# A long-convolution and token-mixing kernel: an inverse transform centred in time, half sums shared by mirrored outputs, and 16-bit sine and cosine

## Chip, cores and metric

The kernel runs on one core of one Trainium2 chip. The metric is the device time of one execution in microseconds (us); shorter is better. Engines are called by the profile's names: PE (TensorE, its weight loads shown apart as PEld), DVE (VectorE), ACT (ScalarE), POOL (GpSimd) and SP (SyncE, which here only issues DMAs).

## What is computed

Two steps follow each other, for a batch of B = 8 sequences of S = 5696 tokens with D = 128 channels:

```
Xf = rfft(x, n=2*S, axis=1); Hf = rfft(h, n=2*S, axis=0)
y  = irfft(Xf * Hf[None], n=2*S, axis=1)[:, :S]         # causal convolution, each channel by itself

theta = y @ w_theta                                     # 128 x 128
zr, zi = y * cos(theta), y * sin(theta)
m = einsum('ts,bsd->btd', w_tok_r, zr) + einsum('ts,bsd->btd', w_tok_i, zi)   # two 5696 x 5696 matrices
u = y + m
out = u + relu(u @ w_ch)
```

## The kernel before

**Three parts in time.** First comes a set-up of tables and the transform of h, to about 55 us in the profile. Then the convolution is done in eight groups (two sequences times 64 channels each), to about 400 us. The last part, from about 410 us, is the mixing with the two token matrices.

**Stages of a group.** A 2S-point transform is split into factors of 89 or 90 and 64.

- Stage A: matmuls L242 (180 columns) with evictions L251 on ACT and L249 on DVE.
- Stage B: twelve chunks. `f2` (L262, L268) makes the spectrum of a chunk in PSUM; ACT casts it to the tile `xs` (L398); DVE multiplies it by the transform of h, the tile `hs`, in one product of 2048 elements, to `uv_t` (L400; the smaller last chunk in two, L405). `hs` is loaded by SP from the DRAM tensor `hf_hbm` (`load`, L391): four loads lead (`LEAD = 4`), and load c + 4 is issued after product c. `uv_t` is what stage C has as weights, in the halves `u_t` and `v_t`.
- Stage C: 16 chunks of 8. Each of the 128 results is a matmul with `u_t` as weights and the table `r_u` streaming (L421), added to one with `v_t` and `r_v` (L422), 128 columns each. A chunk of 1024 columns is evicted to the tile `g` in 16 bits, with a sign per row (`sgn`) on one part: by DVE in one multiplication (L429), or by ACT in two operations (L426, L427), which it does for four of the chunks (eight in the last group).
- Stage D: 64 outputs, two matmuls each (L444, 89 columns, weights from `g`, streaming the table `e_t`). Chunks of 10 outputs are evicted to the tile `yt` by DVE (L448, two chunks) or ACT (L450). The result is stored to `yt_hbm` (L457).

**Order.** `woven` merges lists of steps, each list spread over a share of the stage. Stage C of group g is woven with stage A of group g + 1 (over 0 to 0.7) and with the loads of x for group g + 2 on POOL's queue; stage D of group g is woven with stage B of group g + 1. So two kinds of stages alternate: "C", with A in it, and "B/D". Engines take their instructions in that order. In group 0, the set-up of the rest of the tables (`e_table`) is woven in as well.

**Phases.** `phases_b` makes theta, its sine and cosine, and the products zi and zr. There are 44 steps for rows that come straight from the transform, woven into the last group and following it (`phase_step`, with `turns`), and 46 more, later, among the mixing. In a step, ACT takes the absolute value (L539), the sine (L540) and the cosine of the absolute value (L541), and DVE multiplies (L552, L553). The steps of the transform's rows make a bf16 copy on DVE (L704), which is stored.

**Mixing.** The token matrices are loaded in pieces by POOL's queue (L630), transposed on DVE (L842), partly added (L851), and used in matmuls L1227, L1148 and L1114, with sums on DVE (L1234). Partial results go through DRAM (`cp_hbm`, stored at L977).

Of the kernel before, what the change touches and what calls it, by code (L numbers as in the profile page):

```python
# [10 lines left out]
F32 = mybir.dt.float32  # L11
BF16 = mybir.dt.bfloat16
F16 = mybir.dt.float16
# [4 lines left out]
TWO_PI = 2.0 * math.pi  # L18
# [4 lines left out]
def kernel(  # L23
# [68 lines left out]
    hf_hbm = nc.dram_tensor("hf_hbm", (NCK, 2, N2, 2, HD * CK), F16, kind="Internal").ap()  # L92
# [68 lines left out]
    for n, (col, per) in enumerate(((1, N1), (0, NF), (0, N2), (1, NF))):  # L161
        nc.vector.tensor_scalar(lane[:, n + 2:n + 3], lane[:, col:col + 1], 1.0 / per, None, op0=mult)
# [42 lines left out]
    sign = fc.tile([P, 1], F32)  # L205

# [77 lines left out]
    k_r = index([[0, 2], [1, N2]], "k_r")  # L284
    t_r = []
    for n in range(2):
        t_r.append(s1.tile([P, P], F32, tag=f"t_r{n}", name=f"t_r{n}"))
        for q0 in range(2):
            for q1 in range(2):
                rows, cols = slice(64 * q0, 64 * q0 + 64), slice(64 * q1, 64 * q1 + 64)  # L290
                nc.gpsimd.tensor_scalar(t_r[n][rows, cols], k_r[rows, cols], of_r[rows], 0.25 * (1 + n + q0 - q1),
                                        op0=mult, op1=add)
    for f in load_x(1):
        f()
    e_flat = fc.tile([P, EN * 2 * NB], F16, name="e_t")
# [4 lines left out]
    nc.gpsimd.iota(e_f[1], pattern=[[1, 11], [N2, NB]], base=0, channel_multiplier=0,  # L300
# [4 lines left out]
    signs()  # L305
    pad = v_t[:, 5 * D * CK:6 * D * CK]
# [28 lines left out]
    def h_chunk(c):  # L335
        c0, ck = CHK[c]
        ps = f2(a_h, c, 0)
        h_ = hst[c // 6][:, c % 6]
        dst = h_[:, :, :, :ck]
        if c in (0, 2, 5, 7, 10):  # L340
            nc.vector.tensor_scalar(dst, ps, 16.0 / NF, None, op0=mult)
        else:
            nc.scalar.activation(dst, ps, AF.Copy, scale=16.0 / NF)
        for cc, j in ((0, 0), (NCK - 1, CHK[-1][1] - 1)):
            if c == cc:
                nc.vector.tensor_scalar(dst[:, :, :, j], dst[:, :, :, j], 0.5, None, op0=mult)
        for ri in range(2 if c % 3 == 2 else 0):
            nc.sync.dma_start(
                hf_hbm[c - 2:c + 1, :, :, ri, :].rearrange("c h p n -> p (c h) n"),
                hst[c // 6][64 * ri:64 * ri + 64, c % 6 - 2:c % 6 + 1].rearrange("p c h d k -> p (c h) (d k)"))  # L350

    r_u = fc.tile([P, P], F16)
    r_v = fc.tile([P, P], F16)
    sgn = fc.tile([P, N2], F32)

    def r_table(n_, r_):
        k = within(t_r[n_], s1.tile([P, P], F32, tag=f"k_r{n_}", name=f"k_r{n_}"))
        sine(k, t_r[n_], 1)
        return lambda: (
            nc.vector.tensor_scalar(r_[:, :N2 + EN], k[:, :N2 + EN], 0.125, None, op0=mult),  # L360
            nc.vector.tensor_scalar(r_[:, N2 + EN:], k[:, N2 + EN:], -0.125, None, op0=mult))
# [14 lines left out]
    def s_table():  # L376
        nc.vector.memset(sgn, 1.0)
        nc.vector.tensor_scalar(sgn[:, EN:], sgn[:, EN:], sign, None, op0=mult)
# [3 lines left out]
    def stage_b(a_st, dh, warm=WARM):  # L382

        hs_of = {}

        def load(c):
            if c >= NCK:
                return
            hs = hs_of[c] = fh.tile([P, 2, HD * CK], F16, tag="hs", name="hs")
            for e in range(2):  # L390
                nc.sync.dma_start(hs[64 * e:64 * e + 64], hf_hbm[c, dh])  # L391

        def chunk(c):
            c0, ck = CHK[c]
            hv = hs_of[c].rearrange("p r (d k) -> p r d k", k=CK)
            ps = f2(a_st, c, warm)
            xs = fs.tile([P, 2, HD, CK], F16, tag="xs", name="xs")
            nc.scalar.activation(xs[:, :, :, :ck], ps, AF.Copy)  # L398
            if ck == CK:
                nc.vector.tensor_tensor(  # L400
                    uv[:, :, :, c0:c0 + ck],
                    xs.rearrange("p e d k -> p e (d k)").unsqueeze(1).to_broadcast([P, 2, 2, HD * CK]),
                    hv.rearrange("p r d k -> p r (d k)").unsqueeze(2).to_broadcast([P, 2, 2, HD * CK]), op=mult)
            for r in range(2 if ck < CK else 0):
                nc.vector.tensor_tensor(  # L405
                    uv[:, 2 * r:2 * r + 2, :, c0:c0 + ck], xs[:, :, :, :ck],
                    hv[:, r:r + 1, :, :ck].to_broadcast([P, 2, HD, ck]), op=mult)
            load(c + LEAD)
        return [lambda c=c: load(c) for c in range(LEAD)], [lambda c=c: chunk(c) for c in range(NCK)]

    def stage_c(st, last):
        sg = sgn[:K1].unsqueeze(2).unsqueeze(1).to_broadcast([K1, 2, N2, 8])

        def chunk(q):
# [3 lines left out]
            for i in range(8):  # L418
# [3 lines left out]
                nc.tensor.matmul(o, v_t[:, at:at + P], r_v, start=False, stop=True)  # L422
            g_out = st["g"][:K1, :, q:q + 8].rearrange("p (r n) q -> p r n q", r=2)
            g_in = ps[:K1].rearrange("p a (q r n) -> p r n (a q)", q=4, r=2)
            if q % 16 == 0 and (last or q >= 64):
                nc.scalar.activation(g_out[:, :, :EN], g_in[:, :, :EN], AF.Copy)  # L426
                nc.scalar.mul(g_out[:, :, EN:], g_in[:, :, EN:], sgn[:K1, EN:EN + 1])  # L427
            else:
                nc.vector.tensor_tensor(g_out, g_in, sg, op=mult)  # L429
        return [lambda q=q: chunk(q) for q in range(0, 2 * HD, 8)]  # L430

    def stage_d(st, bp, dh, then=None):
        def chunk(n0, cn):
# [5 lines left out]
            for j in range(cn):  # L439
                n = n0 + j  # L440
                o = ps[:, j // nq, (j % nq) * NB:(j % nq + 1) * NB]
                for ri in range(2):
                    e_ = e_t[:K1, n, ri, :] if n < EN else e_t[:K1, N2 - n, ri, ::-1]
                    nc.tensor.matmul(o, g_[:K1, ri * N2 + n, :], e_, start=(ri == 0), stop=(ri == 1))  # L444
# [30 lines left out]
    r_rest = [lambda: rr.extend([r_table(0, r_u), r_table(1, r_v)]), lambda: rr[0](), lambda: (rr[1](), s_table())]  # L475
# [30 lines left out]
    def phases_b(ti, y_ap, b0, nb, yT, sb, th_pool, th_tag, zi_eng, turns=None, tags=("red", "mag"), m=P,  # L506
# [5 lines left out]
        red = sb.tile([P, n], F32, tag=(tags or ("red", "mag"))[0], name="red")[:m]  # L512
        mag = sb.tile([P, n], F32, tag=(tags or ("red", "mag"))[1], name="mag")[:m]
        y_ap = y_ap[:m]
        if turns is None:
# [8 lines left out]
        else:  # L524
            ones, plus, minus, w_neg = turns
# [13 lines left out]
        nc.scalar.activation(mag, r, AF.Abs)  # L539
        nc.scalar.activation(red, r, AF.Sin, bias=zero_b[:m], scale=-TWO_PI)  # L540
        nc.scalar.activation(mag, mag, AF.Sin, bias=half_pi[:m], scale=-TWO_PI)  # L541
# [7 lines left out]
        else:  # L549
            zi = red.bitcast(BF16)[:, :n]  # L550
            zr = mag.bitcast(BF16)[:, :n]
        zi_eng.tensor_mul(zi, red, yflat)  # L552
        nc.vector.tensor_mul(zr, mag, yflat)  # L553
# [172 lines left out]
    for g, (bp, dh) in enumerate(groups):  # L726
# [12 lines left out]
        woven((c_, 0.06 if a_ else 0.0, 1.0), (a_, 0.0, 0.7), now, load_, (load_x(g + 2, st), 0.1, 1.02))  # L739
# [550 lines left out]
```

## Time and profile before

| | |
|---|---|
| median of 3 runs | 2061.07 us (2054.74 to 2062.02) |
| profiled execution: span | 2056.1 us (no whole time is given beside it) |
| PE, DVE, ACT, POOL busy | 95%, 77%, 31%, 47% |
| mean granted TensorE clock | 0.99 |
| stage C of the groups 1 to 4, first L421 to last L422 | 19.1, 19.1, 19.1, 20.1 us |
| stage B/D between them | about 19 us |

Times are those of one execution from the start of its span. A line as "L400 DVE" is line 400 of the kernel. A matmul's duration includes its way through the array, so the pace of a stream of matmuls is read from the starts.

### The profile page before, as it was taken

To read this page: it belongs to the slowest core of one execution; us is meant where nothing else is said; L and a number is where in the kernel's file an instruction comes from. 1 tells how busy PE (TensorE), PEld (TensorE's weight loads), DVE (VectorE), ACT (ScalarE), POOL (GpSimd) and SP (SyncE) were. 2 spreads that over 40 slices of the span, in tenths; PEclk is the share of its full clock that TensorE was granted. 3 is DMA by queue.
4 is the path that set the end of the run, shared out by engine and by line. 5 is a ranking of instruction groups with operands and counts; after the bars stand their busy time and mean duration, and the time that the engine had idled before them with its cause. 6 is when DMAs were issued, how large, how long until landed. Compare 5 with 4: busy or idle time off the path is not lost.

```text
span 2056.1 us, 41703 instructions
## 1 busy us (share of the span) xinstructions
PE 1951.6 (95%) x15757; PEld 1077.6 (52%) x15933; DVE 1579.0 (77%) x2802; ACT 640.1 (31%) x972; POOL 969.0 (47%) x1766
## 2 busy tenths in 40 slices
PE   7789889789999999999999998999999999999998
PEld 5688878654444444444444443444444444444444
DVE  7777778777788888888867667867777686777767
ACT  6778777862332333333300000011111111111111
POOL 8323412385354545445476454454544535354450
PEclk9899999999999999999999999999999999999999
DMA  9899987999899998989899799687887969788783
GB/s 156 125 158 168 148 161 215 235 271 199 164 171 183 166 180 157 178 167 184 163 174 163 118 246 222 104 153 132 148 147 128 155 127 153 131 150 146 133 153 86
DMA packets 504250, 335.02 MB, mean 163 GB/s; under 512 B 184759, under 2 KB 457271, under 8 KB 503063
## 3 DMA queue, kind: packets, MB, share of 16 engines
q0 software_dynamic: 322368, 157.47, 59.9%
q1 hardware_dynamic: 175696, 163.33, 27.5%
q10 hardware_dynamic: 5984, 11.54, 1.6%
q8 instruction: 125, 2.05, 0.4%
q14 instruction: 77, 0.63, 0.1%
HBM read 376.39 MB, written 92.49 MB: 228 GB/s over the span
## 4 chain that ended last, share of the span: by engine, by line
PE 60%; DVE 5%; DMA 4%; POOL 2%; issue 2%; ACT 0%; DVEq 0%; ACTq 0%; POOLq 0%; SPq 0%
PE m L1227 56%; POOL ring L630 2%; DVE c L1234 2%; DMA ring<-in_moe_w_tok_i_dram 2%; DVE b L783 1%; PE v L929 1%; PE utp L922 1%; DMA b<-z_hbm 1%; PE m L1231 1%; DVE wt L842 1%; DMA ring<-in_moe_w_tok_r_dram 1%; PE theta_ps L517 0%; PE tpz L870 0%; DMA yT<-yt_hbm 0%; PE m L1114 0%
## 5 line engine op out<-in xcount | busy, mean ns | idle before, releaser
L630 POOL DMA_DIRECT2D ring<-in_moe_w_tok_i_dram x720 | 387.9, 546 | 662.4 <-DVE wt L842 567.0
L630 POOL DMA_DIRECT2D ring<-in_moe_w_tok_r_dram x720 | 386.5, 548 | 149.8 <-DVE wt L842 84.7
L842 DVE STREAM_TRANSPOSE wt<-ring 128x384 f32<-128x384 f32 (+2 forms) x720 | 358.7, 522 | 116.4 <-PE m L1227 69.5
L1227 PE MATMUL m<-b,wt 128*128 128x512 bf16 x1605 | 386.6, 380 | 3.8 <-DVE wt L842 1.7
L1227 PEld LDWEIGHTS <-wt 128*128 128x128 bf16 x1804 | 176.4, 98 | 219.8 <-DVE wt L842 7.5
L1234 DVE TENSOR_TENSOR c<-c,m 128x512 f32<-128x512 f32 x412 | 264.9, 668 | 0.4 <-PE m L1227 0.4
L924 ACT ACTIVATE ring<-utp 128x512 bf16<-128x512 bf16 x85 | 50.8, 597 | 582.2 <-PE utp L922 582.2
L421 PE MATMUL ps<-r_u,uv_t 128*128 128x128 f16 x1024 | 125.6, 219 | 9.1 <-DVE uv_t L405 3.0
L422 PE MATMUL ps<-r_v,uv_t 128*128 128x128 f16 x1024 | 124.6, 219 | 1.3 <-issue 0.9
L400 DVE TENSOR_TENSOR uv_t<-xs,hs 128x2048 f16<-128x2048 f16 x88 | 105.7, 1224 | 23.4 <-ACT xs L398 12.5
L1148 PE MATMUL m<-b,wt 128*128 128x512 bf16 x471 | 111.6, 383 | 10.1 <-DVE wt L842 4.9
L919 ACT ACTIVATE ub<-c 128x512 bf16<-128x512 f32 x88 | 55.1, 628 | 193.0 <-DMA ring<-in_moe_w_tok_r_dram 114.6
L146 POOL DMA_DIRECT2D x<-in_x_dram x128 | 99.6, 786 | 22.6 <-POOL x L144 13.3
L422 PEld LDWEIGHTS <-uv_t 128*128 128x128 f16 x1024 | 100.0, 98 | 9.3 <-issue 7.7
L398 ACT ACTIVATE xs<-ps 128x1024 f16<-128x1024 f32 x96 | 91.7, 977 | 37.8 <-DVE uv_t L400 23.0
L421 PEld LDWEIGHTS <-uv_t 128*128 128x128 f16 x1024 | 100.1, 98 | 4.5 <-DVE uv_t L405 4.3
L1148 PEld LDWEIGHTS <-wt 128*128 128x128 bf16 x528 | 50.5, 98 | 67.5 <-DVE wt L842 7.3
L519 ACT ACTIVATE red<-theta_ps,magic 128x512 f32<-128x512 f32 (+1 forms) x46 | 31.6, 687 | 135.7 <-PE theta_ps L517 106.6
L262 PEld LDWEIGHTS <-w_t 64*128 64x128 f16 x3240 | 58.1, 99 | 29.2 <-issue 21.7
L872 ACT ACTIVATE ring<-tpz 128x512 bf16<-128x512 bf16 (+1 forms) x46 | 27.5, 597 | 130.4 <-PE tpz L870 114.9
L541 ACT ACTIVATE mag<-mag,half_pi 128x512 f32<-128x512 f32 (+1 forms) x90 | 65.1, 723 | 0.0
L242 PE MATMUL ps<-f_t,x 89*128 89x180 f16 x512 | 60.3, 252 | 2.3 <-DVE a L249 1.2
(2929 smaller groups left out, 3758.7 us busy)
## 6 DMA issues: line engine op xcount, KB each, us to landing
ring<-in_moe_w_tok_r_dram POOLq DMA_DIRECT2D x352, 96.0 KB, 4.3
ring<-in_moe_w_tok_i_dram POOLq DMA_DIRECT2D x352, 96.0 KB, 4.8
ring<-in_moe_w_tok_r_dram POOLq DMA_DIRECT2D x352, 80.0 KB, 4.4
ring<-in_moe_w_tok_i_dram POOLq DMA_DIRECT2D x352, 80.0 KB, 3.8
hs<-hf_hbm SPq DMA_DIRECT2D x192, 128.0 KB, 3.4
cp_hbm<-c SPq DMA_DIRECT2D x88, 256.0 KB, 2.3
c<-cp_hbm SPq DMA_DIRECT2D x88, 256.0 KB, 4.2
out_dram<-c SPq DMA_DIRECT2D x88, 256.0 KB, 4.2
```

What stands on the lines that cost most here:

```text
L146: nc.gpsimd.dma_start(x16[p0:p1, e, n0:n0 + 16, :HD], bass.AP(tensor=src.tensor, offset=src.offset + (p0 * N2 + n0) * D + dh * HD, ap=[[N2 ...
L242: nc.tensor.matmul(ps[:, i // 2, (i % 2) * 2 * K1:(i % 2 + 1) * 2 * K1], lhs(q + i), f1_t[:NB], start=True, stop=True)
L398: nc.scalar.activation(xs[:, :, :, :ck], ps, AF.Copy)
L400: nc.vector.tensor_tensor(uv[:, :, :, c0:c0 + ck], xs.rearrange("p e d k -> p e (d k)").unsqueeze(1).to_broadcast([P, 2, 2, HD * CK]), hv. ...
L421: nc.tensor.matmul(o, u_t[:, at:at + P], r_u, start=True, stop=False)
L422: nc.tensor.matmul(o, v_t[:, at:at + P], r_v, start=False, stop=True)
L541: nc.scalar.activation(mag, mag, AF.Sin, bias=half_pi[:m], scale=-TWO_PI)
L630: nc.gpsimd.dma_start(wb[32 * i:32 * i + 32, :ng, :nj * 64], bass.AP(tensor=a.tensor, offset=a.offset + row0 * S + p * H + i * QR + j0 * 6 ...
L842: nc.vector.transpose(wt.rearrange("p j t r -> p (j t r)").bitcast(F32).rearrange("p (j g t) -> p g j t", j=TJ, g=4)[:, :ng, :nj], wb[:, : ...
L1148: nc.tensor.matmul(ms[n // 2 * 2 + h], a[n][:, j, :, r], bts_of[p][jj][n % 2 * 2 + h][:, r, :], start=(n % 2 == 0 and jj == 0 and r == 0), ...
L1227: nc.tensor.matmul(ms[q], a[q][:, j, :, r], bts[jj][q][:, r, :], start=(jj == 0 and r == 0), stop=(jj == NJ - 1 and r == 1 and q not in left))
L1234: nc.vector.tensor_tensor(c, z, ms[q], op=op)
```

## The change

The inverse transform is centred in time: output n and its mirror at 64 - n have tables that differ by signs only. For 14 pairs (`NP = 14`) stage C makes half sums instead of whole results, and stage D adds them to one output and subtracts them for the other.

- `r_v` has 100 columns instead of 128, and its matmul adds only to the last 100 columns of a result; the first 28 columns of a result come from `r_u` alone, and the last 28 columns of `r_u` are zero. The eviction has no sign any more: DVE copies, and ACT takes one activation of 1024 elements, for the chunks q = 24, 56, 88 and 120 instead of 64, 80, 96 and 112 (the last group keeps its eight).
- Stage D asks `terms_of` for its matmuls: four for each of 28 outputs, two for each of 36. For the four, a negated half of the odd rows of `e_t` is kept in `e_neg`, made once by POOL (`e_minus`, in group 0).
- Stage A of the next group is woven over 0 to 0.88 of C instead of 0.7.
- `hf_hbm` holds the spectrum of h once, with the two parts in the two halves of the partitions. It is stored by 4 DMAs of 128 rows instead of 8 of 64. A load of `hs` is three DMAs, one straight (128 rows of 1 KB) and two that swap the halves (64 rows of 1 KB), instead of two of 64 rows of 2 KB: 288 instead of 192 in all.
- The tables are made with other offsets (`lane`, `t_r`, iotas), by a few more and smaller operations; `sgn` is gone.
- In the phases, sine and cosine are written in 16 bits, so that the products have 16-bit operands only. In the steps with `turns` the order is sine, absolute value, cosine, the absolute value is written in place to PSUM, and the cosine reads it.

```diff
-    hf_hbm = nc.dram_tensor("hf_hbm", (NCK, 2, N2, 2, HD * CK), F16, kind="Internal").ap()
+    NP = 14
+    ND = N2 - 2 * NP
+    RC = 2 * NP + 2 * ND
...
+    hf_hbm = nc.dram_tensor("hf_hbm", (NCK, 2, P, HD * CK), F16, kind="Internal").ap()
...
-        for ri in range(2 if c % 3 == 2 else 0):
+        if c % 3 == 2:
             nc.sync.dma_start(
-                hf_hbm[c - 2:c + 1, :, :, ri, :].rearrange("c h p n -> p (c h) n"),
-                hst[c // 6][64 * ri:64 * ri + 64, c % 6 - 2:c % 6 + 1].rearrange("p c h d k -> p (c h) (d k)"))
+                hf_hbm[c - 2:c + 1].rearrange("c h p n -> p (c h) n"),
+                hst[c // 6][:, c % 6 - 2:c % 6 + 1].rearrange("p c h d k -> p (c h) (d k)"))
...
-    r_v = fc.tile([P, P], F16)
-    sgn = fc.tile([P, N2], F32)
+    r_v = fc.tile([P, RC], F16)
...
-    def s_table():
-        nc.vector.memset(sgn, 1.0)
-        nc.vector.tensor_scalar(sgn[:, EN:], sgn[:, EN:], sign, None, op0=mult)
+    def e_minus():
+        nc.gpsimd.tensor_scalar(e_neg[:K1], e_t[:K1, 1:2 * NP:2], -1.0, None, op0=mult)
...
             hs = hs_of[c] = fh.tile([P, 2, HD * CK], F16, tag="hs", name="hs")
+            nc.sync.dma_start(hs[:, 0], hf_hbm[c, dh])
             for e in range(2):
-                nc.sync.dma_start(hs[64 * e:64 * e + 64], hf_hbm[c, dh])
+                nc.sync.dma_start(hs[64 * e:64 * e + 64, 1], hf_hbm[c, dh, 64 - 64 * e:128 - 64 * e])
...
-                nc.tensor.matmul(o, v_t[:, at:at + P], r_v, start=False, stop=True)
-            g_out = st["g"][:K1, :, q:q + 8].rearrange("p (r n) q -> p r n q", r=2)
-            g_in = ps[:K1].rearrange("p a (q r n) -> p r n (a q)", q=4, r=2)
-            if q % 16 == 0 and (last or q >= 64):
-                nc.scalar.activation(g_out[:, :, :EN], g_in[:, :, :EN], AF.Copy)
-                nc.scalar.mul(g_out[:, :, EN:], g_in[:, :, EN:], sgn[:K1, EN:EN + 1])
+                nc.tensor.matmul(o[:, 2 * NP:], v_t[:, at:at + P], r_v, start=False, stop=True)
+            g_out = st["g"][:K1, :, q:q + 8]
+            g_in = ps[:K1].rearrange("p a (q c) -> p c (a q)", q=4)
+            if (last and q % 16 == 0) or (not last and q % 32 == 24):
+                nc.scalar.activation(g_out, g_in, AF.Copy)
             else:
-                nc.vector.tensor_tensor(g_out, g_in, sg, op=mult)
+                nc.vector.tensor_copy(g_out, g_in)
...
+    def terms_of(n):
+
+        v = abs(n - N2 // 2)
+        c, s = e_t[:K1, v, 0, :], e_t[:K1, v, 1, :]
+        if v % 2 and v < 2 * NP:
+            i = v // 2
+            c_, s_ = (e_neg[:K1, i, r, :] for r in range(2))
+            late = ((s, c_) if n >= N2 // 2 else (s_, c))
+            out_ = [(i, c), (NP + i, s), (RC + i, late[0]), (RC + NP + i, late[1])]
+        else:
+            f = (n - N2 // 2) % N2
+            i = 2 * NP + (f // 2 if f % 2 == 0 else N2 // 2 + (f - 2 * NP) // 2)
+            out_ = [(i, c), (ND + i, s)]
+        return [(i, e if n >= N2 // 2 else e[:, ::-1]) for i, e in out_]
...
-                for ri in range(2):
-                    e_ = e_t[:K1, n, ri, :] if n < EN else e_t[:K1, N2 - n, ri, ::-1]
-                    nc.tensor.matmul(o, g_[:K1, ri * N2 + n, :], e_, start=(ri == 0), stop=(ri == 1))
+                terms = terms_of(n0 + j)
+                for i, (at, e_) in enumerate(terms):
+                    nc.tensor.matmul(o, g_[:K1, at, :], e_, start=(i == 0), stop=(i == len(terms) - 1))
...
-        nc.scalar.activation(mag, r, AF.Abs)
-        nc.scalar.activation(red, r, AF.Sin, bias=zero_b[:m], scale=-TWO_PI)
-        nc.scalar.activation(mag, mag, AF.Sin, bias=half_pi[:m], scale=-TWO_PI)
+        if turns is None:
+            nc.scalar.activation(mag, r, AF.Abs)
+        nc.scalar.activation(sin_, r, AF.Sin, bias=zero_b[:m], scale=-TWO_PI)
+        if turns is not None:
+            nc.scalar.activation(mag, r, AF.Abs)
+        nc.scalar.activation(cos_, mag, AF.Sin, bias=half_pi[:m], scale=-TWO_PI)
...
-        zi_eng.tensor_mul(zi, red, yflat)
-        nc.vector.tensor_mul(zr, mag, yflat)
+        zi_eng.tensor_mul(zi, sin_, yflat)
+        nc.vector.tensor_mul(zr, cos_, yflat)
...
-        woven((c_, 0.06 if a_ else 0.0, 1.0), (a_, 0.0, 0.7), now, load_, (load_x(g + 2, st), 0.1, 1.02))
+        if g == 0:
+            load_ = load_ + [e_minus]
+        woven((c_, 0.06 if a_ else 0.0, 1.0), (a_, 0.0, 0.88), now, load_, (load_x(g + 2, st), 0.1, 1.02))
```

## The prediction

> **What bounds the kernel now.** I read the page first (engines, then the chain), then the stretches of one transform group, then the groups, the waits of tile `hs`, and the timelines of VectorE and TensorE in the groups' stages. Engines and chain:
>
> ```profile
> PE 1951.6 (95%) x15757; PEld 1077.6 (52%) x15933; DVE 1579.0 (77%) x2802; ACT 640.1 (31%) x972; POOL 969.0 (47%) x1766
> PE 60%; DVE 5%; DMA 4%; POOL 2%; issue 2%; ACT 0%; DVEq 0%; ACTq 0%; POOLq 0%; SPq 0%
> ```
>
> The stretches answer better. Here is a stage B/D, then a stage C, then everything from 460 us on (columns: length, then busy time of PE, PEld, DVE, ACT, POOL, granted clock, DMA share, GB/s):
>
> ```profile
> 171.60:190.40 18.80, 15.59 (x513) 13.59 (x511) 16.60 (x16) 15.42 (x19) 4.06 (x8) 1.00 0.92 158
> 190.40:209.50 19.10, 19.03 (x312) 18.83 (x312) 13.61 (x12) 15.02 (x24) 9.33 (x17) 1.00 1.28 169
> 460.00:2056.00 1596.00, 1562.82 (x8005) 741.11 (x8162) 1221.13 (x2372) 289.52 (x474) 775.54 (x1437) 1.00 0.86 157
> ```
>
> Three regimes. From 460 us the token mixing is TensorE's: 1562.8 of 1596.0 us, so the change can touch at most the 33 us of gaps there. Stage C is TensorE's as well (19.03 of 19.10). Stage B/D is not: VectorE is busy 16.60 of 18.80. With a period of about 38.3 us and eight groups, the transform ends near 410 us, with phase steps among its last pieces.
>
> In stage C (152.5 to 171.6 us) TensorE feeds VectorE, which waits:
>
> ```profile
> L421 PE MATMUL ps<-r_u,uv_t 128*128 128x128 f16 x128 | 15.7, 219 | 0.5 <-ACT a__3418 L251 0.5
> L422 PE MATMUL ps<-r_v,uv_t 128*128 128x128 f16 x127 | 15.5, 219 | 0.1
> L429 DVE TENSOR_TENSOR g__3431<-ps,sgn 90x1024 f16<-90x1024 f32 x11 | 13.4, 1220 | 5.2 <-PE ps L422 4.0 <-issue 1.2
> ```
>
> Its matmuls start one behind the other; stage A's and stage D's pace stand beside them (first number start, second length, last count):
>
> ```profile
> 158.03 0.22 PE L422 MATMUL ps<-r_v,uv_t 128*128 128x128 f16 x1
> 158.08 0.22 PE L421 MATMUL ps<-r_u,uv_t 128*128 128x128 f16 x1
> 158.14 0.22 PE L422 MATMUL ps<-r_v,uv_t 128*128 128x128 f16 x1
> 158.86 0.80 PE L242 MATMUL ps<-f_t,x 89*128 89x180 f16 x8
> 175.18 1.02 PE L444 MATMUL ps<-e_t,g__3431 90*128 90x89 f16 x20
> ```
>
> From 158.03 to 158.14 two starts pass: 55.6 ns each at 128 columns. L444 does 20 in 1.02 us, the last lasting 0.20: 43 ns at 89 columns. L242 does 8 in 0.80 us: 80 ns at 180. The pace follows the columns.
>
> In stage B, VectorE's products run almost end to end:
>
> ```profile
> 173.51 1.23 DVE L400 TENSOR_TENSOR uv_t<-xs,hs 128x2048 f16<-128x2048 f16 x1 [0.41 <-ACT xs L398]
> 174.65 1.08 DVE L448 CAST yt<-ps 128x890 bf16<-128x890 f32 x1
> 175.65 3.59 DVE L400 TENSOR_TENSOR uv_t<-xs,hs 128x2048 f16<-128x2048 f16 x3
> ...
> 187.67 2.38 DVE L400 TENSOR_TENSOR uv_t<-xs,hs 128x2048 f16<-128x2048 f16 x2 [0.50 <-ACT xs L398]
> 189.96 0.68 DVE L405 TENSOR_TENSOR uv_t<-xs,hs 128x256 f16<-128x256 f16 x2
> ```
>
> The loads that they need are barely in time (tile `hs`: issue cost on SP; what VectorE waited for; issue to landing):
>
> ```profile
> L391 SPq DMA_DIRECT2D hs<-hf_hbm x192: 444/596/2639, 43.2 to 343.7; - x192
>   ACT xs L398: 13.5, 23
>   DMA hs<-hf_hbm: 11.7, 11
> DMA to landing us min/median/max: 2.4/3.4/11.8
> ```
>
> **The change part by part.** *Stage C, gain.* 128 of a group's 256 matmuls stream 100 columns, not 128. Between the points (89, 43) and (128, 55.6) the pace at 100 is 46.6 ns, saving 9.0; in proportion to columns it is 43.4, saving 12.2. I take 10.5: 128 x 10.5 = 1.35 us a group. The evictions must keep up. VectorE's 12 cost 12 x 1.22 = 14.6 us of 17.7 left; a plain copy is priced by L448, 1078 ns for 890 elements, so 1.24 for 1024: no gain. Scalar's four become one activation of about 1.02 (L398, 1024 elements) where L426 and L427 took 0.61 + 0.67: 0.26 less each, hidden. The new spacing (every fourth chunk) and stage A spread over 0.88 of C keep three evictions (3.66 us) under four chunks' TensorE time (about 4.6). Six steady groups give 6 x 1.35 = 8.1. Group 0's C (70.9 to 92.0) is partly VectorE's, with two chains for the e tables: 0.3. The last C (30.3 us, phase steps inside) 0.5. Total -9, bounds -12 and -3.
>
> The Trainium skill ("TensorE: Matmul & The Clock Gate", Back-to-back issue gap) says that a sustained stream of weight load and matmul is spaced by both, about 81 ns at 128 columns, and (LDWEIGHTS) that a load's time goes by its 128 columns alone. Shorter streams would then save little in C. The trace shows 55.6 ns with a weight load of 98 ns before each matmul, and 43 at 89 columns, so the loads overlap; by the rule this term would be 0.
>
> *Stage D, added matmuls.* 28 mirrored outputs take 4 matmuls, 36 take 2: 184, not 128, so 56 x 43 ns = 2.4 us a group. TensorE's 15.59 of 18.80 us leaves 3.2; cover is thin in busy time, but pipelined matmuls count double there: by starts (360 x 15 ns, 128 x 43, 12 x 163, some stage A) about 13 us. Price 0; uncovered it is 2.4 x 7 = 17.
>
> *Stage B, the loads.* A load is now three DMAs (128 rows of 1 KB, two of 64 rows of 1 KB), not two of 64 rows of 2 KB. SP's issue is 0.53 + 0.60 plus gaps, 1.28 us a load. A 128-row issue takes 0.32 us alone (L977) and is unpriced between 64-row ones; nearest is L391's own 0.44 to 0.53. So 1.6 to 1.81, taken 1.73. Load c+4 is issued when product c is done. From the end of product 0 (174.74) eight loads at 1.73 are issued by 188.6, the last landing about 2.5 after its last issue starts (188.0 + 2.5 = 190.5, up to 191.7 with 3.7), then 0.7 of L405: 191.2 to 192.4 where 190.64 stands. That is +0.6 to +1.8; I take +1.0. A floor is -0.3 (loads covered: Scalar and VectorE as now, one CAST later in the order); a ceiling +2.5, when SP's limit of outstanding DMAs binds (L391's longest issue, 2639 ns, looks like one). The last eviction of C moves from VectorE to Scalar (1.02 where xs 0 could start): +0.3 at most, inside the 1.0. Six stages +6, group 6 to 7 (23.5 us) +1.
>
> *Group 0.* Stores are 4 DMAs of 128 rows instead of 8 (13.8 us on SP) and the first load passes all but one: uv 0 waits there for hs until 54.1, and e-table work ends 51.5, so up to -2.5; the slower loads take it back: -0.3. The negated half e-table is one GpSimd operation of 90x2492, about 2.8 us scaled from a 90x979 one of 1.09; it delays x pieces only, and stage D waits for it in group 0 alone: +0.3 (0 to +2). Set-up tables 100 wide instead of 128, more small operations: 0.
>
> *Phases.* Sine and cosine in 16 bits: a step's two products fall from 684 ns towards 415 (L704, a bf16 copy of 512, takes 417):
>
> ```profile
> L539 ACT ACTIVATE mag<-ps 128x512 f32<-128x512 f32 x22 | 13.7, 622 | 9.2 <-DVE ring L704 9.2
> L553 DVE TENSOR_TENSOR zz<-mag,ring 128x512 bf16<-128x512 f32 x27 | 18.5, 684 | 0.0
> ```
>
> That is VectorE time, and L539's wait shows a step held up before VectorE's copy, which itself waits for stores. Against it, the 44 transform-fed steps now run sine, absolute value, cosine; cosine follows what it needs with no independent operation between, so an overlap of some 0.11 us (a start every 0.48 to 0.61 for lengths of 0.60 to 0.72) is lost, and the absolute value is written back to PSUM: +0.15 us on about 20 steps paced by Scalar, +3. Scalar's eight evictions in the last C give 8 x 0.26 = -2. Net with the relief 0, bounds -4 and +4.
>
> *Mixing.* 46 steps lose 2 x 0.27 us of VectorE, in a stretch that is TensorE's. A few gaps wait for VectorE's L842 and L851: -1, bounds -4 and +2.
>
> **Sum.** C -9, B/D +7, group 0 -0.3 + 0.3, phases 0, mixing -1: -3 us. The profiled span 2056.1 becomes 2053. The profile gives no whole time beside the span; the median of the runs, 2061.07, stands 5.0 above it, and I keep that: 2058. The runs spread over 7 us, so 0.5% (10.3 us: 2050.8 to 2071.4) is about what a measurement of this kernel tells from no change.
>
> **Rivals.** *Loads covered* (0.25): SP overlaps with what VectorE does, hs never ends a wait, B/D stay at 18.8 us, and the relief counts. For it: 11 waits for hs in 104 products total 11.7 us, and the stage shown has none. Against: seven of the eight stages have at least one, so little slack is left. C -9, B/D 0, phases and mixing together -2.5: -11.5, so 2049.5.
> *SP's outstanding DMAs bind* (0.17), the slower side: now 4 loads (8 DMAs) are in flight when the queue is full, afterwards 8 of three a load, 2.7 loads. While landing takes under 1.73 x 8 / 3 = 4.6 us, issue sets the pace; beyond it, landing does. At 5.5 us a load costs 5.5 x 3 / 8 = 2.06, so eight add 2.7 to the 1.0: +3.7 x 7 = +26, with C and mixing +16: 2077. Against: the median landing is 3.4. For: the maximum is 11.8, and in C the DMA share is 1.28.
> *C saves nothing* (0.05), weight loads pacing: +7 - 1 = +6, 2067.
> *Stage D uncovered* (0.05): 2.4 us more on seven stages, +17 - 3 = +14, 2072 or above.
>
> **Numbers.** The forecast keeps 0.48 and 2058. Faster by over 0.5% needs covered loads and a little more: 0.18 of the first rival and 0.07 of the forecast's lower end, 0.25. Slower: 0.15 of the second, 0.04 of the last, 0.01 of the forecast, 0.20. Same: 0.55. The range runs from the first rival with phases and mixing at their gains (-9 - 8 = 2044) to the second at 2077, short of its tail.
>
> **What would show it.** Right: stage C near 17.7 us with starts 45 ns apart on L422's successor; B/D near 19.8 with VectorE waiting on hs rather than xs; 460 us onward as long as now. Wrong: C still 19.1; B/D at or below 18.8 (first rival) or above 21 with SP issues of over 1 us (second); a mixing part that moves by more than 4 us either way.

## The result and the profile after

The changed kernel takes 2084.53 us (median of 6; 2079.62 to 2086.51) where the kernel before, run beside it, takes 2061.55. The ratio is 1.0108, 95% interval 1.0092 to 1.0125: 1.1% slower, and outside the range that was given (2044 to 2077). The profiled spans are 2083.0 and 2056.1, 26.9 us apart. That difference can be read stage by stage from the starts of the first and the last matmul of each stage C ("B/D of groups 0 to 1" is stage D of group 0 woven with stage B of group 1):

| | before | after | difference |
|---|---|---|---|
| first stage C starts | 70.9 | 72.1 | +1.2 |
| the eight stages C, sum | 167.0 | 166.5 | -0.5 |
| B/D of groups 0 to 1 | 22.3 | 33.1 | +10.8 |
| five B/D between groups 1 and 6 | 96.5 | 111.6 | +15.1 |
| B/D of groups 6 to 7 | 23.5 | 27.4 | +3.9 |
| from the end of the last C to the end | 1676.0 | 1672.4 | -3.6 |

So nearly all of it lies in B/D, and stage C, where the gain was expected, brought nothing. The stretches of the changed kernel show both (length, then busy time of PE, PEld, DVE, ACT, POOL, granted clock, DMA share, GB/s). The first is the long B/D, the second the only steady C that kept its clock, then an ordinary B/D, an ordinary C, and the mixing:

```profile
92.50:125.60 33.10, 23.86 (x572) 21.65 (x568) 22.61 (x17) 16.04 (x19) 14.55 (x15) 0.69 0.74 97
125.60:143.50 17.90, 17.82 (x311) 17.44 (x310) 13.32 (x14) 14.38 (x19) 8.12 (x16) 1.00 1.58 174
185.00:207.00 22.00, 18.23 (x572) 15.95 (x568) 16.34 (x17) 17.05 (x20) 4.96 (x9) 1.00 0.80 127
207.00:226.80 19.80, 19.42 (x308) 19.07 (x309) 13.45 (x14) 13.27 (x18) 8.33 (x16) 0.91 1.32 172
460.00:2083.00 1623.00, 1598.23 (x8388) 757.43 (x8385) 1219.71 (x2416) 312.96 (x513) 801.75 (x1485) 1.00 0.87 159
```

C takes 17.9 us at a clock of 1.00, near the 17.7 that the sum had, and 19.8 at 0.91. TensorE's timeline shows where the difference is (start, length):

```profile
208.03 0.21 PE L440 MATMUL ps<-r_v,uv_t 128*128 128x100 f16 x1
208.07 0.22 PE L439 MATMUL ps<-r_u,uv_t 128*128 128x128 f16 x1
208.12 0.21 PE L440 MATMUL ps<-r_v,uv_t 128*128 128x100 f16 x1
...
208.76 0.31 PE L439 MATMUL ps<-r_u,uv_t 128*128 128x128 f16 x1
208.86 0.29 PE L440 MATMUL ps<-r_v,uv_t 128*128 128x100 f16 x1
208.95 0.31 PE L439 MATMUL ps<-r_u,uv_t 128*128 128x128 f16 x1
```

A pair of matmuls starts every 0.10 us at first, every 0.19 us from 208.76 until about 211.6, then every 0.10 again; the four matmuls of stage A between 208.17 and 208.76 are slow as well. The granted clock (third number from the end) shows the same stretch, with the 3.41 us ahead of it:

```profile
204.81:208.22 3.41, 1.98 (x29) 1.60 (x26) 1.83 (x3) 2.39 (x5) 0.00 (x0) 1.00 0.44 118
208.22:211.63 3.41, 3.41 (x35) 3.41 (x33) 2.33 (x2) 1.28 (x2) 1.11 (x2) 0.50 0.60 151
```

A stretch of 3.41 us at half clock costs 1.7 us: 17.9 + 1.7 is 19.6, and the five stages that have one show 19.3 to 20.3. It follows a B/D in which TensorE waited more, 1.35 us of it right ahead of C. In the 3.41 us ahead of the stretch TensorE was busy 1.98 us, and 0.81 to 1.81 us ahead of the other four. No threshold comes out of this: the kernel before was busy 1.76 us from 367.8 to 371.2 and kept its clock. The Trainium skill ("TensorE: Matmul & The Clock Gate", HAM oscillation) says that a wait between bursts of matmuls that crosses a window of about 3.4 us brings the clock down to half. The stretch here has the length of that window, but the longest wait in the 3.41 us ahead of it was 1.35 us, so here shorter waits were enough. The kernel before had all its steady stages C at 1.00.

The waits of tile `hs` after, to be set against those before (issue cost on SP with minimum, median and maximum; the products; what VectorE waited for):

```profile
L410 SPq DMA_DIRECT2D hs<-hf_hbm x192: 444/594/2992, 37.8 to 374.1; - x192
L408 SPq DMA_DIRECT2D hs<-hf_hbm x96: 319/530/2938, 37.4 to 372.4; - x96
L419 DVE TENSOR_TENSOR uv_t<-xs,hs x88: 1214/1226/7126, 53.2 to 375.1; 128x2048 f16<-128x2048 f16 x88
  DMA hs<-hf_hbm: 34.6, 34
  ACT xs L417: 20.3, 16
DMA to landing us min/median/max: 2.0/3.0/10.4
```

VectorE waits for loads three times as long as before (34.6 us, was 11.7), though a DMA lands sooner after its issue (3.0, was 3.4). SP is the one that falls behind. Load c + 4 may go when product c is done. In the B/D from 185.0 to 207.0 product 3 ended at 192.99, and load 7 began at 194.53. These are SP's issues for three of its eight loads:

```profile
191.93 0.98 SPq L408 DMA_DIRECT2D hs<-hf_hbm  x1
192.95 1.48 SPq L410 DMA_DIRECT2D hs<-hf_hbm  x2
194.53 0.53 SPq L408 DMA_DIRECT2D hs<-hf_hbm  x1
195.11 2.03 SPq L410 DMA_DIRECT2D hs<-hf_hbm  x2
...
202.87 0.53 SPq L408 DMA_DIRECT2D hs<-hf_hbm  x1
203.46 1.49 SPq L410 DMA_DIRECT2D hs<-hf_hbm  x2
```

The eight loads take from 188.62 to 204.95, so 2.04 us each. Two issues of L410 take 1.08 us when nothing lengthens them, but some take 1.45 to 2.03.

And one product lasted 7126 ns where the others last 1226. In the long B/D, VectorE and GpSimd stand beside each other so:

```profile
94.84 10.64 DVE L419 TENSOR_TENSOR uv_t<-xs,hs 128x2048 f16<-128x2048 f16 x4 [1.21 <-ACT xs L417]
```
```profile
95.09 6.55 POOL L396 TENSOR_SCALAR e_t<-e_t 90x2492 f16<-90x2492 f16 x1
```

The slow product lies over GpSimd's negation of half the e table (`e_minus`).

### The profile page after: what moved, and what is told of

It reads as the page before. It is cut to its first block, busy times and chain, and to the rows that moved or that the text cites. A ratio compares the mean times of both kernels' runs of the same rounds, so it can differ in the third digit from the quotient of the medians.

```text
span 2083.0 us, 42942 instructions
## 1 busy us (share of the span) xinstructions
PE 1982.1 (95%) x16381; PEld 1098.0 (53%) x16381; DVE 1543.9 (74%) x2805; ACT 639.5 (31%) x936; POOL 972.4 (47%) x1770
## 3 DMA queue, kind: packets, MB, share of 16 engines
q1 hardware_dynamic: 189456, 163.34, 27.7%
## 4 chain that ended last, share of the span: by engine, by line
PE 65%; DVE 3%; DMA 3%; issue 1%; POOL 1%; ACT 0%; DVEq 0%; ACTq 0%; SPq 0%
PE m L1266 60%; DVE b L822 1%; DVE c L1273 1%; DMA ring<-in_moe_w_tok_r_dram 1%; PE v L968 1%; PE utp L961 1%; PE m L1270 1%; DMA b<-z_hbm 1%; DVE wt L881 1%; POOL ring L667 1%; PE theta_ps L551 0%; PE tpz L909 0%; DMA wl<-in_moe_w_tok_i_dram 0%; PE m L1187 0%; PE m L1153 0%
## 5 line engine op out<-in xcount | busy, mean ns | idle before, releaser
L419 DVE TENSOR_TENSOR uv_t<-xs,hs 128x2048 f16<-128x2048 f16 x88 | 111.6, 1292 | 51.7 <-DMA hs<-hf_hbm 32.4
L440 PE MATMUL ps<-r_v,uv_t 128*128 128x100 f16 x1024 | 121.4, 214 | 1.2 <-DVE uv_t L424 1.0
L439 PEld LDWEIGHTS <-uv_t 128*128 128x128 f16 x1024 | 104.4, 102 | 12.5 <-DVE uv_t L424 12.1
L151 POOL DMA_DIRECT2D x<-in_x_dram x128 | 99.6, 785 | 22.8 <-POOL x L149 14.7
L440 PEld LDWEIGHTS <-uv_t 128*128 128x128 f16 x1024 | 103.9, 102 | 9.2 <-issue 6.2
L248 PE MATMUL ps<-f_t,x 89*128 89x180 f16 x512 | 66.0, 261 | 3.1 <-DVE a L255 1.4
L822 DVE TENSOR_TENSOR b<-b 128x1024 bf16<-128x1024 bf16 x100 | 61.4, 684 | 0.0
```

The costliest lines, as they stand in the source:

```text
L151: nc.gpsimd.dma_start(x16[p0:p1, e, n0:n0 + 16, :HD], bass.AP(tensor=src.tensor, offset=src.offset + (p0 * N2 + n0) * D + dh * HD, ap=[[N2 ...
L248: nc.tensor.matmul(ps[:, i // 2, (i % 2) * 2 * K1:(i % 2 + 1) * 2 * K1], lhs(q + i), f1_t[:NB], start=True, stop=True)
L419: nc.vector.tensor_tensor(uv[:, :, :, c0:c0 + ck], xs.rearrange("p e d k -> p e (d k)").unsqueeze(1).to_broadcast([P, 2, 2, HD * CK]), hv. ...
L439: nc.tensor.matmul(o, u_t[:, at:at + P], r_u, start=True, stop=False)
L440: nc.tensor.matmul(o[:, 2 * NP:], v_t[:, at:at + P], r_v, start=False, stop=True)
L822: return [lambda f=f, x=x: f(*x) for f, x in ((nc.vector.tensor_sub, (bt[M3], b12, b22)), (nc.vector.tensor_sub, (bt[M4], b21, b11)), (nc. ...
```

## The experiments

Two theories came out of this: **theory 1**, GpSimd's operation holds VectorE up; **theory 2**, SP's issue of three DMAs a load paces B/D. Against them stood **theory 3**, the 56 added matmuls of stage D pace it. Ratios are to the kernel before, run beside each.

**The negation on ACT** (in the changed kernel):

```diff
-        nc.gpsimd.tensor_scalar(e_neg[:K1], e_t[:K1, 1:2 * NP:2], -1.0, None, op0=mult)
+        nc.scalar.mul(e_neg[:K1], e_t[:K1, 1:2 * NP:2], -1.0)
```

> The changed kernel, with the negated half of the e table made by ACT instead of GpSimd. Theory 1 (GpSimd's 6.55 us operation on two SBUF operands holds VectorE up: one product takes 7.13 us instead of 1.23 while it runs): the longest product falls to about 1.3 us, the first B/D stage from 33.1 us to about 26, and the time by 6 to 8 us, to about 2077. Rival (the first B/D stage is long because of its loads and of the clock): the product still lasts over 5 us, or the stage stays above 31 us, and the time moves by under 2 us.

Measured: 2080.3 us, ratio 1.0076 (1.0057 to 1.0095), so 0.32% or 6.6 us less. The first B/D is 24.1 us.

```profile
L419 DVE TENSOR_TENSOR uv_t<-xs,hs x88: 1211/1225/1309, 52.8 to 362.6; 128x2048 f16<-128x2048 f16 x88
```
```profile
89.45 2.28 ACT L396 ACTIVATE e_t<-e_t 90x2492 f16<-90x2492 f16 x1
```

No product is longer than 1309 ns now, and the same 90x2492 elements take ACT 2.28 us. Theory 1 holds. The Trainium skill ("SBUF — State Buffer", Who interferes with whom) says that a VectorE instruction with two inputs in SBUF contends with a GpSimd instruction that reads SBUF, because they share a port. A product of `xs` and `hs` is one, and 7.13 us beside 6.55 us agrees.

**Two DMAs a load** (in the changed kernel, each 64 rows times two pieces of 1 KB):

```diff
-            nc.sync.dma_start(hs[:, 0], hf_hbm[c, dh])
-            for e in range(2):
-                nc.sync.dma_start(hs[64 * e:64 * e + 64, 1], hf_hbm[c, dh, 64 - 64 * e:128 - 64 * e])
+            halves = hf_hbm[c, dh].rearrange("(r p) n -> p r n", r=2)
+            nc.sync.dma_start(hs[:64], halves)
+            nc.sync.dma_start(hs[64:], halves[:, ::-1])
```

> The changed kernel, with each load of hs as two DMAs of 64 rows times two pieces of 1 KB instead of three. Theory 2 (SP's issue of three DMAs, 1.75 us a load, paces the B/D stages): the pace falls to about 1.3 us a load, B/D of groups 1 to 5 fall from 22.3 to about 20 us, the waits for hs from 34.6 us to under 15, and the time by 13 to 18 us. Rival (SP is not it: pieces of 1 KB take the DMA engines as long, or stage D's 56 added matmuls pace the stage): issue gets shorter but B/D stay above 21.5 us and the time moves by under 4 us.

Measured: 2073.1 us, ratio 1.0039 (1.0025 to 1.0053): 14 us less by the ratios, waits for hs 26.8 us. Most steady stages C are back at 17.9. B/D of groups 1 to 5 are uneven, 19.6 to 25.8, and the waits are far from the 15 us that were expected. So theory 2 holds in direction, but not its 20 us for each stage.

**Two terms in stage D** (in the changed kernel):

```diff
-                terms = terms_of(n0 + j)
+                terms = terms_of(n0 + j)[:2]
```

> The changed kernel, with two matmuls for every output of stage D (128 instead of 184 a group): the two late terms of the 28 mirrored outputs are left out. Theory 3 (the added matmuls stand between the chunks of stage B on TensorE and delay them): B/D of groups 1 to 5 fall from 22.3 us by 1.5 to 2.4, the time by 10 to 17 us. Rival (loads pace the stage, TensorE has room): B/D stay within 0.5 us, the time within 3 us.

Measured: 2082.0 us, ratio 1.0087 (1.0072 to 1.0102), B/D of groups 1 to 5 from 21.4 to 22.9. The gain is 0.2%, about 4 us, and the two intervals overlap: near the rival, far from theory 3.

**Loads left out** (in the changed kernel; the counterpart in the kernel before is below):

```diff
+            if c >= LEAD:
+                hs_of[c] = hs_of[c - LEAD]
+                return
             hs = hs_of[c] = fh.tile([P, 2, HD * CK], F16, tag="hs", name="hs")
```

> The changed kernel, with only the first four loads of hs in each group; the eight later chunks use those four again, so their factors are other ones. Theory 2 (loads): B/D of groups 1 to 5 fall to about 19 us, no wait for hs is left in them, stage C loses its stretch at half clock (19.7 to about 17.9) if that comes from TensorE's waits, time 20 to 30 us less. Theory 3 (matmuls of stage D): B/D stay above 21 us, the time falls by under 8 us.

Measured: 2062.2 us, ratio 0.9999 (0.9985 to 1.0012): 22 us less, as much as the change had lost. B/D of groups 1 to 5: 19.9, 18.7, 24.2, 18.9, 20.3 us; stage C 17.9 to 19.0. So the loads weigh far more than the matmuls of stage D; how much of the 22 us the kernel before pays as well is seen below. The stage of 24.2 us had no load to wait for; TensorE stood still there for 2.12 and 1.68 us with nothing that the profile shows to wait for ("issue"), and then ran at half clock.

**Three DMAs in the kernel before** (the suspected cost alone):

```diff
-            for e in range(2):
-                nc.sync.dma_start(hs[64 * e:64 * e + 64], hf_hbm[c, dh])
+            nc.sync.dma_start(hs[:64], hf_hbm[c, dh])
+            for r in range(2):
+                nc.sync.dma_start(hs[64:, r], hf_hbm[c, dh, :, r])
```

> The kernel before, with each load of hs as three DMAs (64 rows of 2 KB and twice 64 rows of 1 KB) instead of two; nothing else. Theory 2: SP's pace goes from 1.28 to about 1.75 us a load and costs 2 to 3 us in each B/D stage, so 14 to 24 us: 2075 to 2085, most of what the change lost. Rival (the loss needs the change's other parts): B/D within 0.7 us of before, time within 5 us.

Measured: 2094.8 us, ratio 1.0175 (1.0155 to 1.0196), 34 us more, beyond what was expected.

```profile
  DMA hs<-hf_hbm: 37.4, 43
```
```profile
182.70:205.50 22.80, 15.90 (x512) 13.79 (x509) 16.81 (x15) 16.70 (x20) 4.00 (x7) 0.95 0.73 119
205.50:226.80 21.30, 20.96 (x312) 20.64 (x312) 13.82 (x12) 14.16 (x22) 9.41 (x18) 0.89 1.20 164
```

Here the kernel before shows the same picture: waits for hs 37.4 us, B/D of 22.8, and a C of 21.3 at clock 0.89 behind it, where 19.1 at 1.00 stood. One DMA more per load is enough for a loss of that size, and part of it falls due in stage C.

**One DMA a load** (in the changed kernel, negation on ACT; the first half is stored again behind the second, so that the swapped half is the same rows 64 further down):

```diff
...
-            nc.sync.dma_start(hs[:, 0], hf_hbm[c, dh])
-            for e in range(2):
-                nc.sync.dma_start(hs[64 * e:64 * e + 64, 1], hf_hbm[c, dh, 64 - 64 * e:128 - 64 * e])
+            o = hf_hbm[c, dh]
+            nc.sync.dma_start(hs, bass.AP(tensor=o.tensor, offset=o.offset, ap=[[HD * CK, P], [64 * HD * CK, 2], [1, HD * CK]]))
```

> The changed kernel with the negation on ACT, and each load of hs as one DMA of 128 rows times two pieces of 1 KB: the spectrum's first half is stored a second time behind the others, so that the swapped half is the same rows 64 further down (8 stores instead of 4 in group 0). Theory 2 (SP's issue and the three landings pace the B/D stages): with one issue of about 0.6 us a load the B/D stages fall to 19 to 20.5 us, the waits for hs under 10 us; 2055 to 2063. Rival (the 1 KB pieces or the DMA engines pace it, as two DMAs brought only 7 to 8 us): B/D stay above 21, 2068 or more.

Measured: 2057.3 us, ratio 0.9982 (0.9971 to 0.9993).

```profile
L410 SPq DMA_DIRECT2D hs<-hf_hbm x96: 355/360/2865, 47.5 to 348.9; - x96
  ACT xs L417: 26.9, 25
  DMA hs<-hf_hbm: 11.9, 11
DMA to landing us min/median/max: 2.5/3.7/11.7
```

The issue of a whole load costs 0.36 us. The same bytes in the same pieces of 1 KB land later (3.7 us), and yet the waits fall to 11.9 us: it was the issue. B/D of groups 1 to 5 are 18.8 to 21.3 us, a little above what was expected. Theory 2 stands, and its rival with the size of the pieces falls. The Trainium skill ("DMA: Bandwidth & Descriptors", Rules for kernel authors) advises one transfer of 128 partitions over two to disjoint halves; the runs agree for a queue that issues them back to back.

**One DMA in the kernel before, by reading rows twice:**

```diff
-            for e in range(2):
-                nc.sync.dma_start(hs[64 * e:64 * e + 64], hf_hbm[c, dh])
+            o, w = hf_hbm[c, dh], 2 * HD * CK
+            nc.sync.dma_start(hs, bass.AP(tensor=o.tensor, offset=o.offset, ap=[[0, 2], [w, N2], [1, w]]))
```

> The kernel before, with each load of hs as one DMA of 128 rows of 2 KB that reads the 64 stored rows twice, instead of two of 64 rows; nothing else. Theory 2 (SP's issue paces B/D already before the change, a little): waits for hs 11.7 us and B/D of groups 1 to 5 19.3 us fall, to about 18.8; time 3 to 8 us less, 2053 to 2058. If so the changed kernel with the same cure (2057) owes its lead to the loads and not to the transform. Rival (loads are hidden before): within 2 us of before.

Measured: 2400.3 us, ratio 1.1654 (1.1632 to 1.1675). A miss of another kind:

```profile
L391 SPq DMA_DIRECT2D hs<-hf_hbm x96: 482/5173/9777, 44.9 to 663.5; - x96
  DMA hs<-hf_hbm: 344.8, 71
```

B/D took 56 to 63 us. The pattern that leads with a step of zero and a count of 2 made the loads slow: from a doubled copy ("The same cure in the kernel before", below) one DMA of the same size costs SP 0.32 us. So the run says nothing on the question asked. The Trainium skill ("DMA: Bandwidth & Descriptors", Rules for kernel authors) states that the outermost size decides how many of the 16 DMA engines a transfer uses, and that a leading broadcast of c copies confines it to c. That would be 2 of 16 here. A load of 5.17 us agrees with it in direction; no run here shows the engines by themselves.

**16-bit sine and cosine alone, in the kernel before** (the change's text of the phases, cut):

```diff
-        nc.scalar.activation(mag, r, AF.Abs)
-        nc.scalar.activation(red, r, AF.Sin, bias=zero_b[:m], scale=-TWO_PI)
-        nc.scalar.activation(mag, mag, AF.Sin, bias=half_pi[:m], scale=-TWO_PI)
+        nc.scalar.activation(sin_, r, AF.Sin, bias=zero_b[:m], scale=-TWO_PI)
+        if turns is not None:
+            nc.scalar.activation(mag, r, AF.Abs)
+        nc.scalar.activation(cos_, mag, AF.Sin, bias=half_pi[:m], scale=-TWO_PI)
```

> The kernel before with the 16-bit sine and cosine alone, in the change's order. Theory A (the phases and the mixing gain what the products' time falls by): 3 to 6 us less, to about 2056. Theory B (VectorE is not the bound there, and the new order costs ACT 0.15 us a step): within 3 us of before.

Measured: 2058.9 us, ratio 0.9995 (0.9984 to 1.0006). No difference that can be told; theory B.

**Loads left out and the negation on ACT:**

> The changed kernel with the negation on ACT and only the first four loads of hs in each group, whose factors the eight later chunks use again. Theory: the two losses add up, so 2062 minus 7, about 2054 to 2056, with B/D at 19 to 20 us, stage C at 17.9. Rival (they share the same time): within 2 us of 2062.

Measured: 2048.4 us, ratio 0.9945 (0.9928 to 0.9963). The two losses add up, and somewhat more: 0.54%, about 11 us, below the run with loads left out alone, where the negation by itself had brought 6.6. B/D of groups 1 to 5 are 18.7 to 22.6 us, less even than expected.

**Loads left out in the kernel before** (the same edit):

> The kernel before with only the first four loads of hs in each group, whose factors the eight later chunks use again: the counterpart of the same cut in the changed kernel (2048.4 with the negation on ACT). Theory (the transform part of the change is worth about 1.3 us a stage C, once loads are out of the way): B/D 18.5 to 19, C 19.1, time 2054 to 2058. Rival (stage D's added matmuls take back what C gains): 2046 to 2050.

Measured: 2049.2 us, ratio 0.9952 (0.9934 to 0.9970), the rival's number: without loads, and with the negation on ACT, the two kernels are alike within their intervals. The loads cost the kernel before 0.5% as well, so of the 22 us above about 10 are not the change's. By the ratios, the 1.08% of the change divides as follows: 0.61% for what the loads cost it beyond that (1.09 less 0.48), 0.54% for the negation, taken out last, and nothing that can be told for the rest, in which the gain of stage C and the costs of stage D stand against each other.

**128 columns again in stage C** (in the kernel with one load DMA):

```diff
...
-                nc.tensor.matmul(o[:, 2 * NP:], v_t[:, at:at + P], r_v, start=False, stop=True)
+                nc.tensor.matmul(o, v_t[:, at:at + P], r_w, start=False, stop=True)
```

> The kernel of the run with one load DMA, but the second table of stage C streams 128 columns again, the first 28 of them zero; all else stays. Theory (TensorE's streamed columns set stage C): each C is 1.3 to 1.5 us longer, steady ones about 19.3 where 17.9 stood, and the time 8 to 12 us more, 2065 to 2069. Rival (weight loads or evictions set C): C within 0.4 us, time within 3 us.

Measured: 2062.0 us, ratio 1.0016 (1.0002 to 1.0030); six steady stages C of 19.1 us each where 17.9 to 18.4 stood. Against 0.9982 that is 0.34%, 7.0 us: the columns set stage C, at a little less than expected.

**One DMA a load, the second copy made late** (negation on ACT; two load DMAs in group 0 and for the first four loads of group 1):

```diff
...
+            if g == 1 and c == LEAD - 1:
+                for k in range(0, NCK, 3):
+                    nc.sync.dma_start(hf_hbm[k:k + 3, :, P:], hf_hbm[k:k + 3, :, :64])
```

> The changed kernel with the negation on ACT, 4 stores as in the change, two load DMAs in group 0 and for the first four loads of group 1, and then one DMA of 128 rows; the second copy of the half spectrum is made by four DMAs within DRAM after those loads. Against the run with one load DMA (first C starts at 76.4 us where 70.9 to 72.1 stood): the start comes back to about 71, so 4 to 6 us less, 2051 to 2054. Rival (the stores within DRAM delay the x loads or group 1 instead): 2057 or more.

Measured: 2052.75 us, ratio 0.9963 (0.9951 to 0.9975), faster than both kernels. The first C starts at 68.8 us instead of 76.4, and the later stages C keep their clock:

```profile
150.30:168.20 17.90, 17.83 (x312) 17.55 (x312) 13.33 (x13) 14.32 (x19) 8.48 (x16) 1.00 1.62 169
187.50:205.40 17.90, 17.83 (x312) 17.56 (x312) 13.33 (x13) 14.26 (x19) 8.53 (x16) 1.00 1.53 171
```

**The same cure in the kernel before** (a second copy of the 64 rows within DRAM, one DMA of 128 rows of 2 KB):

```diff
-            for e in range(2):
-                nc.sync.dma_start(hs[64 * e:64 * e + 64], hf_hbm[c, dh])
+            if g == 0 or (g == 1 and c < LEAD):
+                for e in range(2):
+                    nc.sync.dma_start(hs[64 * e:64 * e + 64], hf_hbm[c, dh, :N2])
+            else:
+                nc.sync.dma_start(hs, hf_hbm[c, dh])
+            if g == 1 and c == LEAD - 1:
+                for k in range(0, NCK, 3):
+                    nc.sync.dma_start(hf_hbm[k:k + 3, :, N2:], hf_hbm[k:k + 3, :, :N2])
...
```

> The kernel before, with one load DMA of 128 rows of 2 KB from a second copy of the spectrum made by four DMAs within DRAM, two load DMAs in group 0 and for the first four loads of group 1: the counterpart of the run with the late copy in the changed kernel (2052.75). Theory (the lead over the kernel before is the loads'): waits for hs under 6 us, B/D 18.8 to 19.2, 2050 to 2054, no slower than the changed kernel. Rival (the transform earns its 1.2 us a stage C): 2056 to 2060, slower than 2052.75 by 4 or more.

Measured: 2062.1 us, ratio 0.9999 (0.9989 to 1.0009). The theory fell, and the rival holds in direction, with a time above its 2060: with the same kind of loads the changed kernel is 0.36% faster (0.9963 against 0.9999), about 7.5 us. Waits for hs are 6.5 us. B/D of the middle groups came to 18.8 to 19.4 us, but the stage of groups 0 to 1 (24.0) and that of groups 6 to 7 (27.7) took the gain back. In the profiles of the two runs, the eight stages C together are 7.6 us shorter in the changed kernel and its seven B/D 3.0 us longer. Without loads the two kernels came out alike, so what the new transform earns by itself lies between nothing and 7.5 us.

**Seven pairs** (in the kernel with the late copy, `NP = 7`):

> The kernel of the run with the late copy, with 7 mirrored pairs instead of 14: the second matmul of stage C streams 114 columns, stage D has 156 matmuls. Theory (C gains in proportion to the columns saved, B/D loses with D's matmuls): C 18.5 us, B/D about 1 us less, the sum within 3 us of 2052.75, 2050 to 2054. Rival (only C counts): 2056 to 2059.

Measured: 2055.3 us, ratio 0.9974 (0.9961 to 0.9987). Steady C 18.5 us but for one of 19.0, B/D 18.9 to 21.4 in groups 1 to 5. It lies between the two forecasts, and its interval meets that of 14 pairs.

**Loads left out, two terms in stage D** (negation on ACT):

> The changed kernel with the negation on ACT, only the first four loads of hs in each group (reused by the later chunks), and two matmuls for every output of stage D, the late terms left out. Theory (once loads do not pace B/D, stage D's added matmuls do, most where TensorE lost its clock in a stall): B/D go from 18.7 to 22.6 us (mean 20.1 in groups 1 to 5) to 18.8 each, PE clock 1.00 in them, time 6 to 11 us less than 2048.4, about 2038 to 2042. Rival (stalls of TensorE's own instruction stream make B/D uneven, whatever D holds): B/D still up to 22, time within 3 us of 2048.

Measured: 2045.8 us, ratio 0.9920 (0.9904 to 0.9937), 0.25% or 5 us below the run with all terms, with intervals that overlap. Theory 3 has a small share at most. But B/D still vary, 19.1 to 20.8 us. The stretches of two of them, and what TensorE waited for in the first:

```profile
126.00:146.50 20.50, 16.80 (x514) 14.65 (x510) 16.48 (x16) 15.85 (x19) 5.27 (x9) 0.92 0.62 49
164.40:183.50 19.10, 16.07 (x514) 13.71 (x510) 16.37 (x16) 15.71 (x19) 4.89 (x9) 1.00 0.58 47
```
```profile
PE ps L268 <- issue: 2.7, 2, 2.4
```

The long one holds 2.7 us in which TensorE's own instruction stream stood still, and then a clock of 0.92. The traces show what comes ahead of such a stall. The profile has a DMA queue that it calls "instruction"; one transfer of 16 KB on it runs from 126.88 to 128.14, and TensorE goes on 1.39 us after its end (first the queue from 126.8 to 128.2, then TensorE):

```profile
q8 instruction: 1, 0.02, 5.6%
```
```profile
129.53 0.29 PE L268 MATMUL ps<-a__2360,w_t 64*128 64x64 f16 x8 [2.36 <-issue]
```

In the traces of all 17 kernels, 45 stalls of 1.25 us or more lie between 70 and 400 us, and 44 of them end 1.26 to 1.74 us after such a transfer. With some 50 transfers in these 330 us, a time picked at random would do so in about one case of fourteen. So TensorE waits there, by all that the timing shows, for its own instructions to arrive; no run changes these transfers, so the cause is not tested. The stalls are in the kernel before as well (12.0 us in all from 70 to 380 us, 11.6 in this run), where they left the steady B/D within 18.8 to 19.7. Why the changed kernel's B/D are less even stays open.

## Why the prediction was wrong, point by point

- **Stage B, the loads (+1.0 a stage, +7 in all).** The step that failed most. The chain was right: the issue of eight loads on SP, then the last landing, then L424. Its term for the pace was too small: 1.73 us a load in the sum, 2.04 to 2.32 in the six B/D behind the first, from the start of the first of the eight to the end of the last (SP was busy for 1.80 to 2.14 of it). With 2.04 the prediction's own chain ends at 207.5 in the stage shown (188.6 + 8 x 2.04 - 0.6 + 2.5 + 0.7), and it ended at 207.35. The sum took usual issues of 0.53 and 0.60 us and left out the long ones, though 29 of the 160 issues in the kernel before from 85 us on last over 1 us; 37 of 240 do so afterwards. B/D grew by 2.2 to 3.9 us (10.8 in groups 0 to 1, with the negation), above the ceiling of 2.5 in most. Loads left out bring 22 us back, of which the kernel before has about 10 as well.
- **The slower rival's number.** It gave nearly the right time (2077) and nearly the right pace (2.06 us a load), but by another way, so that is luck: it needed landings of over 4.6 us with a full queue, and the median landing is 3.0. Of the 44 issues over 0.7 us, 19 began with at most two DMAs of `hs` in flight, so no limit of that kind is seen; what lengthens them stays open.
- **Stage C (-9).** The mechanism was right: 17.9 us at full clock, and 7.0 us in the run with full columns. It was taken back, -0.5 in all: later loads left TensorE waiting, and a half-clock stretch that costs 1.7 us landed in five stages. The sum had no term for a loss of clock in C. With one load DMA all steady stages C are back at 17.9 to 18.4. The rule of the Trainium skill that was weighed there ("TensorE: Matmul & The Clock Gate", Back-to-back issue gap), that weight loads would pace the stream, is not what happened: a pair of 128 and 100 columns starts every 0.10 us.
- **The negated table (+0.3).** Wrong twice. The duration, scaled from a smaller operation, was 2.8 us and measured 6.55. And its cover was named wrongly ("it delays x pieces only"): it held VectorE's product up for 5.9 us. It cost 6.6 us, and 11 us in the runs without loads. No run shows how long the operation takes on GpSimd without VectorE beside it.
- **Stage D (0; 17 uncovered).** 4 to 5 us, by the two runs with two terms, each with an interval that meets its counterpart's: mostly covered. That rival's price slipped in its sum: it added +14 to the forecast of 2058, where the median of 2061 was meant, so 2072 should read 2075.
- **Group 0 (-0.3).** The first C starts 1.2 us later. In the three runs with loads left out it starts at 67.6 to 69.5, which points at the slower loads: they took more than the sum gave them.
- **Phases 0 and mixing -1.** From the end of the last C on, the changed kernel is 3.6 us shorter, inside the bounds. The phases alone show no difference, so which part earns it stays open.

## What to carry to other kernels

Cost the issue of a DMA on its queue as work, and compare its pace with that of the stage that eats the data: one DMA more per load was enough for 34 us. Take the mean of the issues in the trace, long ones included, not the usual one. A copy kept in the order in which it is read repaid its making in the changed kernel (0.9963), but brought nothing in the kernel before (0.9999). A stage that leaves TensorE waiting can be paid twice, once there and once in the half clock after it (1.7 us here), so price a wait ahead of a TensorE stage with both. Before putting an operation on an idle GpSimd, look at which VectorE instructions with two inputs in SBUF run beside it.

## What was not expected of the hardware

- A GpSimd operation of 6.55 us stretched a VectorE product from 1.23 to 7.13 us.
- A load as one DMA of 128 rows of two 1 KB pieces costs SP 0.36 us, as two of 64 rows 0.57 and 0.61, as three 0.53, 0.44 and 0.59 (medians, or usual values); about one issue in six lasts over 1 us where a load is two or three DMAs.
- A source that leads with a step of zero and a count of 2 made a 256 KB load cost SP 5.2 us (median) and B/D 60 us.
- TensorE stands still for up to 3.3 us with nothing shown to wait for (kernel before with the late copy), and the stalls over 1.25 us end 1.26 to 1.74 us after a 16 KB transfer of the queue "instruction" in 44 cases of 45. Half clock can follow: in the run with loads left out, 30 matmuls of stage D then take 2.44 us instead of 1.42.
